# A Fourier convolution with a routed expert layer: the forward turns of batches 1 and 2 go through HBM

## The chip, the cores and the metric

The kernel runs on one core of a Trainium2 chip. A core has a matrix engine (PE, with its weight load shown as PEld), a vector engine (DVE), a scalar engine (ACT), a general engine (POOL) and a queue engine (SP) that here does nothing but issue transfers. They run side by side and wait for one another through semaphores; 16 DMA engines move data between HBM and the on-chip memory. The metric is the device time of one execution in microseconds (us): the median of three runs.

## What is computed

```python
def _attn_ref(x, filt_r, filt_i):                 # x: 8 batches x 3072 positions x 256 channels
    X = np.fft.rfft(x, axis=1)
    Y = X * (filt_r + 1j * filt_i)[None, :, :]
    return np.fft.irfft(Y, n=x.shape[1], axis=1)

def _moe_ref(x, w_gate, w1, w2, capacity):        # x: 24576 tokens x 256, 8 experts
    logits = x @ w_gate
    expert_idx = np.argmax(logits, axis=1)
    ...
    for i in range(N):                            # the first `capacity` = 768 tokens of an expert
        e = expert_idx[i]
        if counts[e] < capacity:
            disp[e, counts[e]] = x[i]; pos[i] = counts[e]; counts[e] += 1; keep[i] = True
    h = np.maximum(np.einsum('ecd,edf->ecf', disp, w1), 0.0)
    y = np.einsum('ecf,efd->ecd', h, w2)
    ...                                           # out[i] = gate_w[i] * y[expert, pos], else 0
```

Only the first 768 tokens of each of the 8 experts count, so the kernel convolves batches 0, 1 and 2 (the last in part) and turns to the experts; a branch that convolves everything stands behind them for inputs that need it.

## The kernel before

**The transform.** A batch has 3072 = 96 x 32 positions (n1, n2) and 256 channels. The forward transform over n1 is taken for eight **chunks** of four n2 each. `load_x` brings a chunk (96 partitions, 4 x 256 values, 384 KB) into a buffer `xt`, of which there are four. `a(c, h)` multiplies it on PE with the table `A` for one half h of the channels, and `a_out` copies the result on ACT into `ZA[h]`, which has the channels on its partitions. The second transform, over n2, wants (q, n2) on the partitions. `t(k)` makes it so: 16 PE transposes of `ZA` and two ACT copies into `Q`, six times in a batch. `Q` has 24 pairs of frequencies, 128 partitions x 256 channels each.

**The middle.** `middle` is the loop over six groups g of four pairs: `b(g, h)` (PE with table `Bc`, then two products with the filter on DVE and two sums on POOL), `g(u)` (PE with `IG`, a cast `yh` on ACT, a rest `yl` on DVE) and `bi(u)` (PE with `BIh`, `BIl`, copies into `V` on ACT). `g(0)` needs both halves of group 0 and stands behind the four `b` of groups 0 and 1. The argument `first` is a list of steps of which one runs behind each `b`; `fill` is a list of lists of which one runs at each filler, from group 1 on.

**The inverse and the routing.** `ai(V, dst, h)` returns the steps of the inverse transform: 11 for half 0 and 8 for half 1. I call the 8 of half 1 S0 to S7. Each has PE products, one ACT copy into a buffer `rt`, of which there are five, and a store of 153 or 192 KB to `ybuf`. `route` returns the lists `counts` (DVE, the last a scan), one PE step `sums` that waits for that scan, `slots` (DVE), four `masks` (DVE), and `table`: four PE steps, table 0 to 3, and a last one on DVE.

**The order.** It is written out by hand: every engine takes its instructions in the order in which the Python code calls them, and a wait holds up all that stands behind it on that engine. For b = 0 and 1 the loop calls the middle of batch b, then chunks 0 to 3 of batch b+1, the inverse of half 0, chunks 4 to 7 among `counts`, then `sums`, then the six `t` among `slots`, and then

```python
            run([masks[0], masks[1], S[0], S[1], table[0], masks[2], S[2], S[3], table[1], masks[3], S[4], S[5]])
            ahead = S[6:]
            fill = [[table[2]], table[3:]]
```

so S6 and S7 run inside the next middle, as `first`. I call the stretch from the end of a middle to the next one a **turn**; there are two. In the second turn `load_a` also brings 1 MB of expert 0's first weights into `raw`, and `cut_a` splits them on ACT in four pieces, from the first filler of the last middle on. All transfers named here but those of `cut_a` are issued by SP.

Of the kernel before, what the change touches and what calls it, by code (L numbers as in the profile page):

```python
# [9 lines left out]
F32 = mybir.dt.float32  # L10
# [11 lines left out]
N1, N2, NP = 96, 32, 24  # L22
# [67 lines left out]
def fftconv_moe_kernel(ctx, tc, x, x0, fr, fi, fny, wg, w1, w2, ca, cai, cb, co, out, cap):  # L90
    nc = tc.nc
    NB, SEQ, D = x.shape[0], N1 * N2, 256
# [4 lines left out]
    NB0 = min(NB, -(-E * cap // SEQ) + 1)  # L97
# [11 lines left out]
    dram = ctx.enter_context(tc.tile_pool(name="dram", bufs=1, space=bass.MemoryType.DRAM))  # L109
# [48 lines left out]
    def interleave(*lists):  # L158

        marks = sorted(((i + 1) / (len(l) + 1), j, i) for j, l in enumerate(lists) for i in range(len(l)))  # L160
        for _, j, i in marks:
            lists[j][i]()

    def run(fs):
        for f in fs:
            f()

    class Conv:
# [81 lines left out]
                f(self.A[k * 32:(k + 1) * 32, c, 32:4 * QP], t[N1:, k * w:(k + 1) * w])  # L250

        def load_x(self, b, c):
            t = self.side.tile([N1, 4, D], F32, name="xt", tag="xt")
            src = x[b] if isinstance(b, int) else x[bass.ds(b, 1)].rearrange("o c a t d -> (o c) a t d")
            nc.sync.dma_start(out=t, in_=src[c])
            self.xts[c] = t
# [541 lines left out]
    cv = Conv(p1b, top, side, True)  # L798
    route_tiles(p1b)

    with tc.manual_schedule():

        V = new_V(vp)
# [13 lines left out]
        ps = bank()  # L817
# [21 lines left out]
        fill, ahead = [[cv.finish_low]], [lambda: (cv.t(3), cv.t(4)), lambda: None, lambda: cv.t(5)]  # L839
        nz = -(-len(zfill) // (NB0 - 1))  # L840

        def with_zeros(fill, at):
            fill = [list(f) for f in fill] + [[] for _ in range(10 - len(fill))]
            for i in range(nz):
                fill[at[i % len(at)]].append(lambda: zero_out(1))
            return fill

        def rows_in(b, cs, more):
            steps = []
            for c in cs:  # L850
                steps += [lambda c=c: cv.a(c, 0), lambda c=c: cv.a(c, 1)]
                if more:
                    steps.append(lambda c=c: cv.load_x(b, c + 4))
            return steps

        for b in range(NB0 - 1):
            for c in range(4):
                cv.load_x(b + 1, c)
            cv.middle(V, with_zeros(fill, (3, 6)), ahead)
            L = new_L()  # L860
            halves = [ai(V, ybuf[b], h, L) for h in range(2)]
            counts, sums, slots, masks, table = route(L, False, (ohp, ohp))
            for q in range(4):
                ti(V, q)
            run(rows_in(b + 1, range(4), True))
            run(halves[0])
            interleave(rows_in(b + 1, range(4, 8), False), counts)
            sums()
            interleave([lambda k=k: cv.t(k) for k in range(NP // 4)], slots)
            if b + 2 == NB0:  # L870
                side_ctx.close()
                w0 = run_ctx.enter_context(tc.tile_pool(name="w0", bufs=1, side="right"))
                raw0 = run_ctx.enter_context(tc.tile_pool(name="raw0", bufs=1, side="right"))
                ep = run_ctx.enter_context(tc.tile_pool(name="ep", bufs=1, side="right"))
                (load_a, cut_a), (load_b, cut_b) = (load_part(0, part, raw0, w0, 4) for part in "ab")
                load_a()
            S = halves[1]
            run([masks[0], masks[1], S[0], S[1], table[0], masks[2], S[2], S[3], table[1], masks[3], S[4], S[5]])
            ahead = S[6:]
            fill = [[table[2]], table[3:]]  # L880


        b = NB0 - 1
        sm["p"] = ep
        last_fill = last_constants(ep)
# [14 lines left out]
        def early_row(e, t):  # L900
            gather(early_x[e][:, t:t + 1, :], idx0, e * NT + t, 1, b * SEQ)

        fill[0].append(cut_a[0])
        fill[1] += [early_index, cut_a[1]]
        fill += [[cut_a[2], lambda: early_row(0, 0)], [cut_a[3], load_b, lambda: early_row(0, 1)], [lambda: early_row(0, 2)], [last_fill],
                 [cut_b[0]], [cut_b[1]], [cut_b[2]], [cut_b[3], lambda: early_gate(0)]]
        cv.middle(V, fill, ahead, last=[early_turn])
        top_ctx.close()
# [94 lines left out]
        with tc.If(least < cap):  # L1003
            with ExitStack() as gp:
# [7 lines left out]
                V = new_V(p1b)  # L1012
# [91 lines left out]
```

## Time and profile before

| | us |
|---|---|
| median of 3 runs | 493.52 (492.25 to 494.03) |
| the profiled execution, its own time | 489.18 |
| its span, from the first to the last instruction | 487.5 |
| PE busy | 476.7 (98% of the span) |
| ACT busy | 269.3 (55%) |
| DVE busy | 239.7 (49%) |
| POOL busy | 199.9 (41%) |

The trace is of one execution, and its times are from the start of the span; 1.7 us lie around the span. Matmuls are pipelined, so a row's duration reaches a little into the next; the distance between the starts of two rows is what the first cost. A float32 product on PE counts as two instructions. TensorE's granted clock was 0.998 of full speed over the span.

### The profile page before, as it was taken

To read this page: it belongs to the slowest core of one execution; us is meant where nothing else is said; L and a number is where in the kernel's file an instruction comes from. 1 tells how busy PE (TensorE), PEld (TensorE's weight loads), DVE (VectorE), ACT (ScalarE), POOL (GpSimd) and SP (SyncE) were. 2 spreads that over 40 slices of the span, in tenths; PEclk is the share of its full clock that TensorE was granted. 3 is DMA by queue.
4 is the path that set the end of the run, shared out by engine and by line. 5 is a ranking of instruction groups with operands and counts; after the bars stand their busy time and mean duration, and the time that the engine had idled before them with its cause. 6 is when DMAs were issued, how large, how long until landed. Compare 5 with 4: busy or idle time off the path is not lost.

```text
span 487.5 us, 10394 instructions
## 1 busy us (share of the span) xinstructions
PE 476.7 (98%) x4078; PEld 469.7 (96%) x4078; DVE 239.7 (49%) x533; ACT 269.3 (55%) x626; POOL 199.9 (41%) x246
## 2 busy tenths in 40 slices
PE   8999999999999999999999999999999999999994
PEld 8999999999999999998999999999999999999994
DVE  3587755777737878956432342332322422423510
ACT  3555767456667677664362684392382572673411
POOL 3064210444100885617632654354463462563022
PEclk9999999999999999999999999999999999999999
DMA  8996180890546458385738599989989979984001
GB/s 292 377 323 263 34 233 5 218 377 13 162 107 190 88 154 185 82 227 99 222 73 234 128 240 267 356 231 260 364 216 271 378 191 278 374 162 107 0 24 48
DMA packets 60186, 95.70 MB, mean 196 GB/s; under 512 B 4224, under 2 KB 36704, under 8 KB 60000
## 3 DMA queue, kind: packets, MB, share of 16 engines
q1 hardware_dynamic: 43472, 63.28, 40.0%
q0 software_dynamic: 15344, 29.56, 28.1%
q10 hardware_dynamic: 1312, 2.10, 1.4%
q8 instruction: 34, 0.56, 0.5%
q14 instruction: 24, 0.20, 0.1%
HBM read 54.82 MB, written 40.11 MB: 195 GB/s over the span
## 4 chain that ended last, share of the span: by engine, by line
PE 73%; issue 10%; POOL 6%; ACT 4%; DMA 3%; DVE 2%; POOLq 0%; SPq 0%; DVEq 0%
PE ps L610 21%; PE ps L661 19%; PE ps L268 9%; PE ps L407 6%; PE ps L337 6%; PE ps L304 5%; PE ps L351 4%; POOL y L667 2%; DMA raw<-w 2%; PE ps L291 1%; PE ps L584 1%; POOL rows L570 1%; ACT Q L296 1%; DMA V<-x 1%; POOL wal L702 1%
## 5 line engine op out<-in xcount | busy, mean ns | idle before, releaser
L661 PE MATMUL ps<-wbh,h 128*128 128x256 f32 x768 | 139.6, 282 | 0.0
L593 DVE SCALAR_TENSOR_TENSOR h<-ps,h 128x384 fp32r<-128x384 f32 x128 | 67.0, 552 | 109.0 <-ACT h L591 108.7
L661 PEld LDWEIGHTS ps<-wbh,h 128*128 128x128 f32 x768 | 118.9, 189 | 0.8 <-issue 0.4
L661 PE MATMUL ps<-wbl,h 128*128 128x256 f32 x384 | 107.6, 280 | 0.0
L667 POOL DMA_INDIRECT y<-ob,idxs x48 | 48.1, 1003 | 115.7 <-ACT ob L664 110.5
L610 PE MATMUL ps<-xl,wah 128*128 128x384 f32 x256 | 86.4, 338 | 0.3 <-DVE xl L595 0.2
L610 PE MATMUL ps<-xh,wah 128*128 128x384 f32 x256 | 86.5, 338 | 0.0
L610 PE MATMUL ps<-xh,wal 128*128 128x384 f32 x256 | 86.2, 337 | 0.0
L591 ACT ACTIVATE h<-ps 128x384 fp32r<-128x384 f32 x128 | 58.8, 497 | 33.7 <-PE ps L610 32.5
L661 PEld LDWEIGHTS ps<-wbl,h 128*128 128x128 f32 x384 | 72.5, 189 | 0.0
L664 ACT ACTIVATE ob<-ps,gt 128x256 f32<-128x256 f32 x48 | 22.7, 475 | 85.4 <-PE ps L661 45.7
L324 POOL TENSOR_TENSOR t<-t,t 128x256 f32<-128x256 f32 x33 | 24.9, 754 | 68.3 <-DVE t L320 44.3
L570 POOL DMA_INDIRECT rows<-ybuf,idxg x42 | 42.4, 1009 | 16.3 <-issue 11.0
L610 PEld LDWEIGHTS ps<-xl,wah 128*128 128x128 f32 x256 | 48.0, 188 | 0.9 <-DVE xl L595 0.9
L610 PEld LDWEIGHTS ps<-xh,wah 128*128 128x128 f32 x256 | 48.0, 188 | 0.2
L610 PEld LDWEIGHTS ps<-xh,wal 128*128 128x128 f32 x256 | 48.0, 188 | 0.0
L595 DVE TENSOR_TENSOR xl<-ps,xh 128x384 fp32r<-128x384 f32 x32 | 16.2, 547 | 46.9 <-ACT xh L591 46.9
L340 ACT CAST yh<-ps 128x408 fp32r<-128x408 f32 x48 | 23.9, 502 | 27.7 <-PE ps L337 26.2
L337 PE MATMUL ps<-IG,t 128*128 128x136 f32 x288 | 38.2, 281 | 0.9 <-POOL t L325 0.9
L337 PEld LDWEIGHTS ps<-IG,t 128*128 128x128 f32 x288 | 35.4, 190 | 1.5 <-POOL t L325 1.5
L304 PE MATMUL ps<-Bc,Q 128*128 128x128 f32 x288 | 35.8, 276 | 0.0
L304 PEld LDWEIGHTS ps<-Bc,Q 128*128 128x128 f32 x288 | 33.8, 192 | 0.1
(134 smaller groups left out, 766.9 us busy)
## 6 DMA issues: line engine op xcount, KB each, us to landing
y<-zt SPq DMA_DIRECT2D x12, 2048.0 KB, 22.0
raw<-w SPq DMA_DIRECT2D x13, 1024.0 KB, 9.9
wbl<-w POOLq DMA_DIRECT2D x16, 512.0 KB, 12.2
wal<-w POOLq DMA_DIRECT2D x14, 512.0 KB, 7.5
xt<-x SPq DMA_DIRECT2D x16, 384.0 KB, 5.2
ybuf<-rt SPq DMA_DIRECT2D x16, 192.0 KB, 2.9
ybuf<-rt SPq DMA_DIRECT2D x20, 153.0 KB, 2.5
Q<-x SPq DMA_DIRECT2D x4, 528.0 KB, 8.9
```

Source lines behind the costliest of these rows:

```text
L268: nc.tensor.matmul(ps[:, i * w:(i + 1) * w], xt[:, i, h * 128:(h + 1) * 128], A[:, i * QP:i * QP + w], start=True, stop=True)
L304: nc.tensor.matmul(ps[:, i * 128:(i + 1) * 128], self.Q[:, p, h * 128:(h + 1) * 128], self.Bc[:, 1 if p == NP - 1 else 0, :], start=True, ...
L324: eng.tensor_tensor(out=t1[:, :, 0, :], in0=t1[:, :, 0, :], in1=t2[:, :, 1, :], op=ALU.subtract)
L337: nc.tensor.matmul(ps[:, i * 136:(i + 1) * 136], self.ysb[(p // 4, h)][:, (p % 4) * 128:(p % 4 + 1) * 128], self.IG[:, h, :], start=True, ...
L340: nc.scalar.copy(fh[:, o], ps[:, :408])
L407: nc.tensor.matmul(ps[:N1, i * w:(i + 1) * w], AI[:, n0 + i, :], V[h][:, :w // 2, n0 + i, :], start=True, stop=True)
L570: nc.gpsimd.indirect_dma_start(out=rows[:, t, :], out_offset=None, in_=yrows[:lim, :], in_offset=bass.IndirectOffsetOnAxis(ap=idx[:, j + t ...
L591: nc.scalar.activation(out=hi, in_=ps, func=AF.Relu if relu else AF.Copy)
L593: nc.vector.scalar_tensor_tensor(out=lo, in0=ps, scalar=0.0, in1=hi.bitcast(F32), op0=ALU.max, op1=ALU.subtract)
L610: nc.tensor.matmul(ps[:, :n * 128], w[:, kk, m * 128:(m + 1) * 128], y[:, kk, o], start=k == 0, stop=k == 5)
L661: nc.tensor.matmul(ps[:, :D], y[:, m, o], w[:, m, :], start=m == 0 and j == 0, stop=m == NF - 1 and j == 2)
L667: ins = nc.gpsimd.indirect_dma_start(out=out, out_offset=bass.IndirectOffsetOnAxis(ap=(idxs if ix is None else ix)[:, j:j + 1], axis=0), i ...
```

## The change

Batches 1 and 2 lose the transposes. `a_rows(c)` multiplies with the operands exchanged, so that the result has q on its partitions and the 256 channels in a row; two ACT copies of 96 x 512 bring it into one of three slots of the former `ZA[0]`, and SP stores it to a new HBM buffer `zturn`. Chunk 7 is stored in two pieces. Seven loads of `Q` read `zturn` back with (q, n2) on the partitions, two of two pairs and five of four. I call them Q0 to Q6. Chunks 4 to 6 of the input are loaded into slots of the former `ZA[1]`, so all input but chunk 7 can be loaded during the middle before. S6 and S7 move ahead of the middle; table 2, table 3 and the last table step become `ahead`. `sums` stands behind two chunks instead of four. `load_a` stands behind Q3 and S5, where it was ahead of S0. The zero stores of the output move from the fillers 3 and 6 to 5 and 7.

```diff
         def load_x(self, b, c):
-            t = self.side.tile([N1, 4, D], F32, name="xt", tag="xt")
+            if self.resident and 4 <= c < NCH - 1:
+                t = self.slot(1, c - 4).rearrange("p (t d) -> p t d", d=D)
+            else:
+                t = self.side.tile([N1, 4, D], F32, name="xt", tag="xt")
...
+        def slot(self, h, k):
+            return self.ZA[h].rearrange("p q t -> p (q t)")[:N1, k * 4 * D:(k + 1) * 4 * D]
+
+        def a_rows(self, c):
+
+            xt, A, z = self.xts.pop(c), self.Ac[c], self.slot(0, c % 3)
+            for k in range(2):
+                ps = bank()
+                for i in range(2):
+                    t = 2 * k + i
+                    nc.tensor.matmul(ps[:QP, i * D:(i + 1) * D], A[:, t * QP:(t + 1) * QP], xt[:, t, :], start=True, stop=True)
+                nc.scalar.copy(z[:, k * 2 * D:(k + 1) * 2 * D], ps[:QP, :])
+                if k or c == NCH - 1:
+                    o = slice(2 * k if c == NCH - 1 else 0, 2 * k + 2)
+                    nc.sync.dma_start(out=zturn[:, c * 4 + o.start:c * 4 + o.stop, :],
+                                      in_=z[:, o.start * D:o.stop * D].rearrange("p (t d) -> p t d", d=D))
+
+        def load_Q(self, p, n):
+
+            src = zturn[p * 4:(p + n) * 4].rearrange("(p j) t c -> (j t) p c", p=n)
+            nc.sync.dma_start(out=self.Q[:, p:p + n, :], in_=src)
...
-            run(rows_in(b + 1, range(4), True))
+            run(rows_in(b + 1, range(4)))
             run(halves[0])
-            interleave(rows_in(b + 1, range(4, 8), False), counts)
+            interleave(rows_in(b + 1, range(4, 6)), counts)
             sums()
-            interleave([lambda k=k: cv.t(k) for k in range(NP // 4)], slots)
+            interleave(rows_in(b + 1, range(6, 8)), slots)
...
-                load_a()
             S = halves[1]
...
+            first = [load_a] if b + 2 == NB0 else []
+            run([Q[0], Q[1], masks[0], masks[1], S[0], S[1], table[0], masks[2], S[2], Q[2], S[3], table[1], masks[3], S[4], Q[3], S[5]] + first + S[6:])
+            ahead = [table[2], lambda: run(table[3:])]
+            fill = []
+            loads = Q[4:]
```

SP's order in the second turn, from the last forward work to the end of the turn, stood before like this (the `raw` row is `load_a`, the 96x4x128 rows are the stores of S0 to S7, `both` is a small constant):

```order
L695 DMA raw<-w 128x2x1024 [waits DVE_49,PE_49,DMAHW7_49,Activation_49,Pool_49]
L413 DMA ybuf<-rt 96x4x128 [waits DMAHW0_49,Activation_49]
L413 DMA ybuf<-rt 96x4x128 [waits DMAHW1_49,Activation_49]
...
L763 DMA both<-co 128x144 [waits DMAHW6_49]
L413 DMA ybuf<-rt 96x4x128 [waits DMAHW7_49,Activation_49]
L413 DMA ybuf<-rt 96x4x128 [waits DMAHW0_49,Activation_49]
```

and in the changed kernel, from the second piece of chunk 7 on (`zturn<-ZA`), it stands like this:

```order
L292 DMA zturn<-ZA_97 96x512 [waits DMAHW7_49,Activation_49]
L298 DMA Q<-zturn 128x2x256 [waits DMAHW5_49,DMAHW6_49,DMAHW4_49,DMAHW7_49,DMAHW3_49,DMAHW0_49]
L298 DMA Q<-zturn 128x2x256 [waits DMAHW1_49]
L439 DMA ybuf<-rt 96x4x128 [waits DMAHW2_49,Activation_49]
L439 DMA ybuf<-rt 96x4x128 [waits Activation_49] x2
L298 DMA Q<-zturn 128x4x256
L439 DMA ybuf<-rt 96x4x128 [waits Activation_49] x2
L298 DMA Q<-zturn 128x4x256 [waits DMAHW0_49]
L439 DMA ybuf<-rt 96x4x128 [waits DMAHW1_49,Activation_49]
L721 DMA raw<-w 128x2x1024 [waits DMAHW2_49,PE_49]
L439 DMA ybuf<-rt 96x4x128 [waits DMAHW3_49,Activation_49]
L439 DMA ybuf<-rt 96x4x128 [waits DMAHW4_49,Activation_49]
```

`load_a` went from ahead of the eight stores to behind four loads of Q and six stores, and all of them stand behind a load that waits for the stores of the last chunks (the DMAHW names).

On PE, the end of the first turn and the start of the middle stood before like this (L407 are steps S, L304 is `b`, L550 a table, L337 `g(0)`):

```order
L407 MATMUL ps<-V_117,AI 96x128 x8
L304 MATMUL ps<-Bc,Q 128x128 x8
L407 MATMUL ps<-V_117,AI 96x128 x4
L304 MATMUL ps<-Bc,Q 128x128 x4
L407 MATMUL ps<-V_117,AI 96x128 x4
L550 LDWEIGHTS ol
L550 MATMUL pr<-ohh,ol 128x96
...
L304 MATMUL ps<-Bc,Q 128x128 x4
L337 MATMUL ps<-IG,t_1272 128x136
```

and the same place in the changed kernel (L433, L330, L576 and L363 are the same four):

```order
L433 MATMUL ps<-V_118,AI 96x128 x16
L330 MATMUL ps<-Bc,Q 128x128 x8
L576 LDWEIGHTS ol
L576 MATMUL pr<-ohh,ol 128x96
...
L330 MATMUL ps<-Bc,Q 128x128 x4
L576 LDWEIGHTS ol
L576 MATMUL pr<-ohh,ol 128x96
...
L330 MATMUL ps<-Bc,Q 128x128 x4
L363 MATMUL ps<-IG,t_1139 128x136
```

Two steps S left the place between the first `b` and `g(0)`, and one more table came into it.

## Rows read from the trace of the kernel before

**Rows 1.** Page, first part: busy time, share of the span, instructions by engine.

```profile
PE 476.7 (98%) x4078; PEld 469.7 (96%) x4078; DVE 239.7 (49%) x533; ACT 269.3 (55%) x626; POOL 199.9 (41%) x246
```

**Rows 2.** Stretches: length, busy PE, PEld, DVE, ACT, POOL, then granted clock, DMA share, GB/s.

```profile
144.30:148.90 4.60, 4.18 (x102) 3.69 (x101) 3.98 (x16) 3.82 (x9) 0.00 (x0) 1.00 0.00 0
190.80:487.00 296.20, 289.82 (x2252) 285.75 (x2250) 111.00 (x274) 149.82 (x296) 131.04 (x128) 1.00 0.75 201
```

**Rows 3.** Timeline of PE, first turn: start, duration, instructions [idle before, released by].

```profile
56.34 7.31 PE L268 MATMUL ps<-A,xt 96*128 96x128 f32 x64
63.48 7.62 PE L407 MATMUL ps<-V,AI 128*96 128x136 f32 x64
70.95 7.31 PE L268 MATMUL ps<-A,xt 96*128 96x128 f32 x64
78.09 0.26 PE L495 MATMUL pr<-sc,tri 96*96 96x8 f32 x2
...
78.45 3.43 PE L291 MATMUL ps<-ident,ZA 64*128 64x64 f32 x81
...
82.74 2.00 PE L407 MATMUL ps<-V,AI 128*96 128x128 f32 x16
84.58 0.51 PE L550 MATMUL pr<-ohh,ol 96*128 96x96 f16 x8
...
88.87 1.95 PE L304 MATMUL ps<-Bc,Q 128*128 128x128 f32 x16
...
94.61 1.55 PE L337 MATMUL ps<-IG,t 128*128 128x136 f32 x12
```

**Rows 4.** Timeline of DVE, first turn: the scan that `sums` waits for.

```profile
74.12 0.69 DVE L491 TENSOR_TENSOR_SCAN sc<-mask,oh 96x256 f32<-96x256 f32 x1
```

**Rows 5.** Timeline of ACT, start of the last middle.

```profile
155.17 0.58 ACT L409 COPY rt<-ps 96x512 f32<-96x512 f32 x1 [0.30 <-PE ps L407]
...
160.08 0.62 ACT L700 CAST wah<-raw 128x512 fp32r<-128x512 f32 x1
160.60 0.63 ACT L704 ACTIVATE wal<-raw 128x512 fp32r<-128x512 f32 x1
161.56 0.50 ACT L340 CAST yh<-ps 128x408 fp32r<-128x408 f32 x1 [0.33 <-PE ps L337]
```

**Rows 6.** Timeline of DVE, last middle: the last table step and what follows it.

```profile
163.29 0.20 DVE L555 TENSOR_TENSOR tacc<-tacc,pr 128x48 f32<-128x48 f32 x1
...
163.90 0.15 DVE L782 TENSOR_TENSOR tot<-tot,lack 128x2 f32<-128x2 f32 x1
```

**Rows 7.** Timeline of PE, second turn and last middle.

```profile
122.39 2.84 PE L268 MATMUL ps<-A,xt 96*128 96x128 f32 x24
...
160.67 1.56 PE L337 MATMUL ps<-IG,t 128*128 128x136 f32 x12
...
170.35 0.50 PE L337 MATMUL ps<-IG,t 128*128 128x136 f32 x2 [0.46 <-POOL t L325]
```

**Rows 8.** Stretches (columns as in Rows 2): rates of single kinds of transfer.

```profile
150.00:151.00 1.00, 1.00 (x17) 0.98 (x15) 0.20 (x1) 1.00 (x4) 0.00 (x0) 1.00 1.01 135
88.00:90.00 2.00, 2.00 (x21) 2.00 (x20) 0.53 (x3) 1.16 (x2) 0.00 (x0) 1.00 1.02 270
266.00:267.00 1.00, 1.00 (x11) 1.00 (x10) 0.83 (x4) 0.83 (x3) 0.00 (x0) 1.00 1.07 341
267.00:268.00 1.00, 1.00 (x11) 1.00 (x10) 0.87 (x4) 0.07 (x1) 0.00 (x0) 1.00 1.06 372
242.00:243.00 1.00, 1.00 (x11) 1.00 (x10) 0.00 (x0) 0.00 (x0) 0.55 (x1) 1.00 1.01 414
30.00:32.00 2.00, 2.00 (x20) 2.00 (x19) 1.75 (x4) 0.97 (x3) 1.77 (x3) 1.00 1.03 256
```

**Rows 9.** SP's timeline at `load_a`, and the landing times of L413's 38 stores.

```profile
149.01 0.41 SPq L695 DMA_DIRECT2D raw<-w  x1
...
DMA to landing us min/median/max: 2.2/2.7/7.9
```

More of the change, by code (lines that the diff above doesn't have):

```diff
@@ L114, in fftconv_moe_kernel @@
     yall = dram.tile([NB, N1, N2, CH], F32, name="yall")
+    zturn = dram.tile([4 * NP, N2, D], F32, name="zturn")
     yrows = ybuf.rearrange("b a t c -> (b a t) c")
@@ L846, in with_zeros, with rows_in @@
             return fill
-        def rows_in(b, cs, more):
+        def rows_in(b, cs):
             steps = []
             for c in cs:
-                steps += [lambda c=c: cv.a(c, 0), lambda c=c: cv.a(c, 1)]
-                if more:
-                    steps.append(lambda c=c: cv.load_x(b, c + 4))
+                steps.append(lambda c=c: cv.a_rows(c))
+                if c == 0:
+                    steps.append(lambda: cv.load_x(b, NCH - 1))
             return steps
+        loads = []
         for b in range(NB0 - 1):
-            for c in range(4):
-                cv.load_x(b + 1, c)
-            cv.middle(V, with_zeros(fill, (3, 6)), ahead)
+            loads += [lambda b=b, c=c: cv.load_x(b + 1, c) for c in range(NCH - 1)]
+            fill = with_zeros(fill, (5, 7))
+            for i, f in enumerate(loads):
+                fill[i // 2].append(f)
+            cv.middle(V, fill, ahead)
             L = new_L()
@@ L875, in fftconv_moe_kernel @@
                 (load_a, cut_a), (load_b, cut_b) = (load_part(0, part, raw0, w0, 4) for part in "ab")
-                load_a()
             S = halves[1]
-            run([masks[0], masks[1], S[0], S[1], table[0], masks[2], S[2], S[3], table[1], masks[3], S[4], S[5]])
-            ahead = S[6:]
-            fill = [[table[2]], table[3:]]
+            Q = [lambda p=p, n=n: cv.load_Q(p, n) for p, n in ((0, 2), (2, 2), (4, 4), (8, 4), (12, 4), (16, 4), (20, 4))]
+            first = [load_a] if b + 2 == NB0 else []
[3 more added lines that the diff above has]
+            loads = Q[4:]
         b = NB0 - 1
@@ L901, in early_row @@
             gather(early_x[e][:, t:t + 1, :], idx0, e * NT + t, 1, b * SEQ)
-        fill[0].append(cut_a[0])
-        fill[1] += [early_index, cut_a[1]]
-        fill += [[cut_a[2], lambda: early_row(0, 0)], [cut_a[3], load_b, lambda: early_row(0, 1)], [lambda: early_row(0, 2)], [last_fill],
+        fill = [[loads[0], cut_a[0]], [early_index, cut_a[1]] + loads[1:], [cut_a[2], lambda: early_row(0, 0)],
+                [cut_a[3], load_b, lambda: early_row(0, 1)], [lambda: early_row(0, 2)], [last_fill],
                  [cut_b[0]], [cut_b[1]], [cut_b[2]], [cut_b[3], lambda: early_gate(0)]]
```

## The prediction

> **What bounds the kernel now.** The first part of the page has PE busy for 98% of the span [rows 1], at a granted clock of 1.00 in all stretches used here [rows 2, 8]. From 190.8 on PE is idle for 6.4 us of 296, most of it the tail behind its last product [rows 2], so what a turn wins on PE's timeline moves the end by as much. I then read PE's timeline of the first turn; the second repeats it 66.05 later, with the same 4.18 of 4.60 busy in its transposes [rows 2, 3, 7]. Read from start to start: chunks 0 to 3 take 7.14, the inverse of half 0 7.47, chunks 4 to 7 7.14, `sums` 0.36, the transposes 4.29, S0 to S5 with two tables 6.13, and from the first `b` to `g(0)` 5.74 [rows 3]. There is hardly a gap, so only work taken off PE, or a wait put on it, counts. One more place matters: in the last middle PE waits 0.46 at 170.35 for a POOL sum [rows 7]; there POOL and DVE set the pace, not PE.
>
> The sum is made on the profiled execution (489.18, span 487.5). It ran 0.9% below the median of 493.52; I subtract its microseconds from the median, since nothing in the sum depends on that difference.
>
> **Part by part, first turn** (times from its start at 56.34).
>
> Transposes removed: 4.29 of PE. Their 12 ACT copies hide behind that today and go with them.
>
> Operands exchanged: per chunk 4 products of 256 columns instead of 8 of 128, the same number of columns. A product needs at least its columns, so the change lies between nothing and the issue cost saved. No row has 256 float32 columns. I take 0.1 per four chunks, 0.2 in a turn (0 to 0.4). ACT's two copies of 96 x 512 cost 0.58 each [rows 5], under the 1.76 that PE needs per chunk, so they hide. A slot comes round after three chunks (5.3), a store lands 2.2 to 2.7 after its issue [rows 9] (those are half as large; 1 more at most), so the slots hide too.
>
> `sums` moved up: PE comes to it at 7.04 + 7.47 + 3.52 = 18.03. The scan it needs ends at 18.47 [rows 4], less the 0.1 saved ahead of it. PE waits 0.34. Nothing hides this, because chunks 6 and 7 are queued behind.
>
> S6 and S7 moved out of the middle: they cost PE 1.84 [rows 3] wherever they stand, but they filled the start of the middle. `g(0)` waits for POOL's sums of group 0, which come after four DVE products in series: 5.74 behind the first `b`. PE's work in that time was four `b`, S6, S7 and table 2. Six steps S at 0.92 leave 0.6 of the 6.13 for two tables, so a table is 0.3 and the four `b` are 3.6. Now it is four `b` and two tables, 4.2, and PE waits 1.54 for POOL.
>
> Sum of the first turn: 4.29 + 0.2 - 0.34 - 1.54 = 2.6 gained, if the loads of Q come in time. Chunk 7 leaves PE at 18.37 + 0.36 + 3.52 = 22.25, its last copy ACT at 22.83. Its store lands about 2.6 later [rows 9], with two more pieces right ahead of it at 256 GB/s, the rate of 96-partition tiles in rows of 4 KB [rows 8]: 25.4. SP then issues Q0. From issue to full DMA share takes 0.95 (149.01 to about 150) [rows 8, 9]. For the rate of Q the nearest row is the load of w2, also in rows of 1 KB: 341 and 372, so 356 [rows 8]. Q0 and Q1 (0.52 MB) take 1.47. From last byte to semaphore I put 0.67 (the shortest store, 2.2, less 0.95 and 0.58 for 157 kB at 270). They land at 28.5; `b` comes at 22.25 + 6.13 + 1.84 = 30.22, so 1.7 are to spare. Q2 stands behind S0 to S2, 0.197 MB each at 270 [rows 8], and lands at 32.2, when `b` of group 1 comes (32.3). Q3 lands at 35.1, ahead of the end of `g(0)` at 37.4 (start 35.96 as below, and the row's 1.55, less a little for its overlap). SP holds the stores of S0 and later until chunk 7 has landed; with five `rt`, S5's copy waits for S0's store (29.2), but PE has seven banks and `yh` comes only at 36.9.
>
> **Second turn.** The same, with 2.6, but `load_a` now stands behind Q0 to Q3 and S0 to S5. These are 1.57 MB at 356, 1.18 MB at 270 and 1.05 MB at 414 (w1 in rows of 4 KB) [rows 8]: 4.42 + 4.37 + 2.56 = 11.35 from 26.35 on, and 0.67 to land, 38.4. The first piece of `cut_a` is queued on ACT ahead of the first two `yh`. Without a wait the `yh` would start 0.89 behind the start of `g(0)` (35.96), at 36.85, so ACT should reach `raw` well before it has landed. Behind ACT stand `yl` on DVE, the index work, the products of group 2, POOL's sums with a gather between them, and the last part of `g(2)`, the product that waits today. In the trace this chain takes 8.79 from the start of `yh` to 170.35 [rows 5, 7]; the table step of 0.61 that stood in it [rows 6] now comes earlier, so 8.18. The two ACT operations of the cut take 1.15 [rows 5]. So `g(2)` goes on at 38.4 + 1.15 + 8.18 = 47.7, against 170.35 - 122.39 = 47.96 today [rows 7]: 0.2 gained instead of 2.6. The gain of the second turn is nearly eaten by the wait for `raw`.
>
> Bounds: with all transfers at 414, 3.80 MB take 9.2, `raw` lands at 36.2 and the turn gains 2.4. With Q at 256, the slowest row of a large load, it lands at 40.1 and the turn loses 1.5. I take 356 because the size of the rows is the same. Input loads and zero stores go on in the middle behind Q; even at 256 GB/s, the lowest rate of a large transfer in the rows, they end before the next turn (2.75 MB of input in 10.7, in a middle of 33.5, 88.87 to 122.39), so I cost them at nothing. Were they late, they would delay the first stores of a turn, which nobody waits for until the slot comes round.
>
> The rows give a store or load a fixed part of 0.95 + 0.67 = 1.6, twice in series here. The Trainium skill ("DMA: Bandwidth & Descriptors", section "Anatomy of one DMA") gives about 2.0 us for it, most of it the receipt of the last write. By that rule `raw` would land 0.8 later and the sum would be 2.1 instead of 2.8, 491.4. The shortest landing here, 2.2 with its data [rows 9], is below what the rule gives for that size (2.4), so the row stands.
>
> Forecast: 2.6 + 0.2 = 2.8, so 493.52 - 2.8 = **490.7**.
>
> **The rivals.**
>
> *`raw` comes early.* If the queue drains faster, or ACT comes to the cut later than I think, only PE's own waits remain: `g(2)` goes on at 36.85 + 8.18 = 45.0, and both turns gain, 2.6 + 2.9 = 5.5: 488.0. It needs `raw` by 35.7. Speaks for it: 414 GB/s exists in the trace [rows 8]. Against: the stores in rows of 512 B, a third of the bytes, run at 270 [rows 8].
>
> *The loads of Q run at half the rate, and it gets slower.* They read rows that were written microseconds ago, among stores; no row shows such a read. At 178 GB/s Q0 to Q3 take 8.84, `raw` lands at 42.8, `g(2)` goes on at 52.1: 4.2 lost in the second turn. In the first, Q2 lands at 35.1 and Q3 at 39.5, which delays `g(0)` by 1.2 and group 2 by 0.9, leaving 0.5. Sum 3.7 lost: 497.2. It decides at about 225 GB/s, where both turns cancel.
>
> *The stores to the new buffer are slow.* If they ran at 128 instead of 256 GB/s, the last four (1.57 MB, from 17.8 on) would land at 30.8, 5.4 late; the first turn would lose 1.1 and the second 5.2: 499.8. Rows of a store lie 32 KB apart there. The Trainium skill ("DMA: Bandwidth & Descriptors", section "Latency and other measured facts") reports such a loss for row distances at large powers of two, from 2 MiB on, while 512 KiB still ran at the full rate. No run so far shows a store with such distances.
>
> *Nothing comes of it.* If POOL's pace, or a wait on `rt` or on a slot, takes back the 2.6 in both turns, the time stays at 493.5.
>
> **How the numbers follow.** Forecast with its bounds (489.0 to 493) 0.55; `raw` early (487.2 to 489) 0.20; Q slow 0.13; stores slow 0.05; nothing 0.07. The range is 487.2 to 495.5: it takes in the first two and the last, and of the slow cases the mildest. A measurement of this kernel can tell 0.5%, 2.5 us, from no change, and the forecast lies at that edge: 0.55 of its own case is beyond it. Faster: 0.20 + 0.30 = 0.50. Slower: most of the two slow cases, less what stays under 496, and nothing else, 0.13. The same: 0.37.
>
> **What would show it.** In the trace after: no transposes after batch 0's; `sums` with a wait of about 0.3; a PE wait of about 1.5 before each of the two `g(0)`; Q0 issued about 25.4 into a turn; the first `wah` of the last middle waiting for the DMA of `raw`, until about 38.4 into its turn; and `g(2)` there with a wait of some 2 us. Wrong would be: `b` waiting for Q (my rate or the landing of chunk 7 is off), or no ACT wait for `raw` (then the time is near 488).

## The result, and the profile after

The changed kernel takes 498.81 us (497.74 to 499.49, four runs) against 493.5 before: a ratio of 1.0098, 95% interval 1.0075 to 1.0120. The medians differ by 5.3 us, and the interval stands for 3.7 to 5.9 more, where a gain of 2.8 was forecast; the time lies outside the stated range of 487.2 to 495.5. One profile below, e4's, is of an execution slower than the others of its kernel, and no reading rests on it.

The first line of the page, and the cores' view (span, mean granted clock), which for the kernel before gave 487.5 and 0.998:

```profile
PE 476.1 (96%) x3758; PEld 459.0 (92%) x3758; DVE 240.2 (48%) x533; ACT 261.2 (52%) x602; POOL 200.1 (40%) x246
core 0: 497.8 us, clock 0.986
```

PE is busy for about as long as before [rows 1], with 320 instructions fewer. So work was taken away, and waits and a lower clock came in.

The first turn on PE's timeline, to be held against [rows 3]:

```profile
56.26 7.07 PE L288 MATMUL ps<-xt,A 96*96 96x256 f32 x32
63.16 7.62 PE L433 MATMUL ps<-V,AI 128*96 128x136 f32 x64
70.62 3.62 PE L288 MATMUL ps<-ZA,A 96*96 96x256 f32 x16
75.72 0.34 PE L521 MATMUL pr<-sc,tri 96*96 96x8 f32 x2 [1.48 <-DVE sc L517]
...
76.08 2.33 PE L288 MATMUL ps<-ZA,A 96*96 96x256 f32 x8
78.20 3.24 PE L288 MATMUL ps<-xt,A 96*96 96x256 f32 x8
...
89.09 1.95 PE L330 MATMUL ps<-Bc,Q 128*128 128x128 f32 x16
...
93.07 1.13 PE L330 MATMUL ps<-Bc,Q 128*128 128x128 f32 x8 [1.69 <-DMA Q<-zturn]
94.04 0.51 PE L576 MATMUL pr<-ohh,ol 96*128 96x96 f16 x8
94.39 1.86 PE L330 MATMUL ps<-Bc,Q 128*128 128x128 f32 x8
96.04 2.51 PE L363 MATMUL ps<-IG,t 128*128 128x136 f32 x12
```

Two waits stand here, 1.48 ahead of `sums` (L521) and 1.69 ahead of the `b` of group 1 (L330). Behind each the same work takes longer than it should. The two chunks from 70.62 on take 3.62, and the next two 5.20, from 76.08 to 81.28 (where L433 starts again); one half of a `b` takes 0.97 from 93.07 on, and the next 1.65 from 94.39 on. The view by stretches says why (columns as in [rows 2]; the column before the last two is the granted clock):

```profile
74.30:75.70 1.40, 0.00 (x0) 0.00 (x0) 1.29 (x3) 0.56 (x1) 0.00 (x0) 1.00 0.84 244
76.10:77.50 1.40, 1.40 (x9) 1.08 (x9) 1.17 (x6) 0.30 (x1) 0.00 (x0) 1.00 0.67 208
77.60:80.80 3.20, 3.20 (x9) 2.06 (x9) 2.96 (x12) 1.34 (x3) 0.00 (x0) 0.50 0.31 81
81.10:84.10 3.00, 3.00 (x33) 2.93 (x32) 1.22 (x4) 1.75 (x3) 0.00 (x0) 1.00 0.49 146
91.40:93.00 1.60, 0.00 (x0) 0.00 (x0) 1.26 (x3) 0.58 (x1) 0.99 (x2) 1.00 1.09 325
94.70:97.40 2.70, 2.70 (x15) 2.70 (x13) 2.47 (x7) 0.00 (x0) 1.48 (x3) 0.50 1.16 317
145.90:149.00 3.10, 3.10 (x8) 1.98 (x7) 2.86 (x13) 1.17 (x2) 0.00 (x0) 0.50 0.41 116
```

TensorE's granted clock falls to 0.50, its 1.2 GHz level, 1 to 2 us after PE has started again, and comes back to 1.00 after some 3.4. It happens twice in the first turn and once in the second. Added up over half-microsecond stretches, each such phase costs 1.71. In the stretches that I read in the trace of before it was 1.00 throughout [rows 2, 8].

The second turn starts at 124.36. Rows of PE, then the first row of the cut on ACT, then the last part of `g(2)` on PE:

```profile
143.76 0.34 PE L521 MATMUL pr<-sc,tri 96*96 96x8 f32 x2 [1.42 <-DVE sc L517]
161.03 1.13 PE L330 MATMUL ps<-Bc,Q 128*128 128x128 f32 x8 [1.60 <-DMA Q<-zturn]
...
166.97 0.62 ACT L726 CAST wah<-raw 128x512 fp32r<-128x512 f32 x1 [6.84 <-DMA raw<-w]
...
175.79 0.50 PE L363 MATMUL ps<-IG,t 128*128 128x136 f32 x2 [0.99 <-POOL t L351]
...
194.48 0.58 PE L610 MATMUL ps<-ident,rows 64*128 64x64 f32 x12
```

The last row, the first transposes of the expert part, serves as a mark: from the start of a turn to the next start, or to this mark, gives the lengths of the two turns, each with the middle behind it. Before they are 66.05 and 66.64 (the mark is at 189.03), after 68.10 and 70.12: +2.05 and +3.48, together +5.53. That is near the difference of the medians. The remaining 4.8 by which the two profiled spans differ lies behind the mark, where nothing was edited. I come to that first.

### The profile page after: what moved, and what is told of

It is laid out like the page before. It is cut to its first block, busy times and chain, and to the rows that moved or that the text cites. A ratio compares the mean times of both kernels' runs of the same rounds, so it can differ in the third digit from the quotient of the medians.

```text
span 497.8 us, 9802 instructions
## 1 busy us (share of the span) xinstructions
PE 476.1 (96%) x3758; PEld 459.0 (92%) x3758; DVE 240.2 (48%) x533; ACT 261.2 (52%) x602; POOL 200.1 (40%) x246
## 4 chain that ended last, share of the span: by engine, by line
PE 53%; issue 20%; POOL 10%; DMA 7%; DVE 4%; ACT 3%; SPq 1%; POOLq 1%; ACTq 0%; DVEq 0%
PE ps L636 13%; PE ps L687 12%; PE ps L363 5%; PE ps L288 5%; PE ps L330 4%; PE ps L377 4%; POOL y L693 4%; PE ps L433 4%; PE ps L272 3%; POOL rows L596 3%; DMA ybuf<-rt 3%; DMA raw<-w 2%; POOL wal L734 1%; DMA Q<-zturn 1%; PE ps L848 1%
## 5 line engine op out<-in xcount | busy, mean ns | idle before, releaser
L330 PE MATMUL ps<-Bc,Q 128*128 128x128 f32 x288 | 36.7, 280 | 4.3 <-DMA Q<-zturn 3.3
L363 PE MATMUL ps<-IG,t 128*128 128x136 f32 x288 | 39.2, 285 | 1.4 <-POOL t L351 1.4
L330 PEld LDWEIGHTS ps<-Bc,Q 128*128 128x128 f32 x288 | 34.5, 195 | 4.9 <-ACT rt L435 3.5
L363 PEld LDWEIGHTS ps<-IG,t 128*128 128x128 f32 x288 | 36.4, 195 | 2.1 <-POOL t L351 2.0
```

What stands on the lines that cost most here:

```text
L330: nc.tensor.matmul(ps[:, i * 128:(i + 1) * 128], self.Q[:, p, h * 128:(h + 1) * 128], self.Bc[:, 1 if p == NP - 1 else 0, :], start=True, ...
L363: nc.tensor.matmul(ps[:, i * 136:(i + 1) * 136], self.ysb[(p // 4, h)][:, (p % 4) * 128:(p % 4 + 1) * 128], self.IG[:, h, :], start=True, ...
```

## The experiments

All kernels but two start from the changed one. Lengths of turns are read from one profile each, as above; the ratios are from timed runs, each against the kernel before on the same chip:

| kernel | turn 1 | turn 2 | ratio to before (95%) |
|---|---|---|---|
| before, first and second profile | 66.05, 66.05 | 66.64, 66.66 | |
| changed, first and second profile | 68.10, 68.26 | 70.12, 71.20 | 1.0098 (1.0075 to 1.0120) |
| e1 `sums` behind three chunks, and e14 the same again | 63.78, 63.20 | 67.18, 67.45 | 0.9987 (0.9961 to 1.0014) |
| e2 13 products of zeros | 70.50 | 70.14 | 1.0158 (1.0111 to 1.0205) |
| e10 6 products of zeros | 65.05 | 69.01 | 1.0065 (1.0041 to 1.0089) |
| e3 chunk 7 loaded later | 68.82 | 71.70 | 1.0180 (1.0127 to 1.0233) |
| e11 without that load | 67.26 | 69.16 | |
| e6 before, steps moved alone | 67.29 | 67.29 | 1.0022 (1.0000 to 1.0043) |
| e5 e1, later cut, S6 and S7 in the middle | 62.96 | 67.99 | 1.0005 (0.9980 to 1.0030) |
| e7 e1, later cut, Q0 to Q3 together | 67.01 | 70.91 | 1.0110 (1.0071 to 1.0148) |
| e8 e1, `load_a` behind Q2 | 63.23 | 65.50 | 0.9998 (0.9971 to 1.0025) |
| e9 e8, S6 and S7 in the middle, and e15 the same again | 62.90, 63.08 | 71.17, 70.13 | 0.9951 (0.9934 to 0.9968), 0.9988 (0.9962 to 1.0014) |
| e12 the same with Q3 ahead of `load_a` | 63.80 | 70.45 | 0.9996 (0.9973 to 1.0019) |

**How much is steady: e0, e13, e14.** The kernel before and the changed one, without an edit.

> The kernel before, unchanged, profiled once more. In the first profile of it the span was 487.5, some 4 below what the timed runs imply, and from the last middle to the end it has hardly a PE wait; the profile of the changed kernel has some 4 us more of waits in that stretch, which no edit touches. Theory: that part differs from execution to execution, so this profile may show waits there too (span 488 to 492), while the two turns stay at 66.05 from start to start. Rival: the late waits come from the change; then this profile repeats 487.5 with no such waits.

Measured: the turns repeat to 0.02, and the part behind the mark is 3.15 longer, with waits such as this one, which the first profile lacked:

```profile
420.13 0.44 PE L610 MATMUL ps<-xh,wah 128*128 128x384 f32 x1 [1.31 <-ACT ob L664]
```

So the expert part differs from execution to execution: behind the mark the seventeen profiles read here, e4's left out, spread from 297.9 to 305.7, in no order that follows the edits. Single spans can't be compared; the turns are steadier. But a turn is also read from one execution, and a phase of half clock comes in some executions and not in others: e9's two turns add up to 1.38 more than before, and its timed ratio is 0.9951. Where a ratio is near 1, the timed runs decide, not the turns.

> The changed kernel, unchanged, profiled once more, on the same chip as the next. Theory A (the waits at `sums` and at the `b` of group 1 are in the order of the work, so they come in each execution; whether the clock falls behind a given wait is not): the two turns again take 67 to 71 each, with waits of 1.4 to 1.5 at `sums` and 1.6 or more at `b`, and the half clock behind most of them. Rival (the first profile caught a bad execution): a sum of the two turns under 135 instead of 138.2.

> The kernel with `sums` behind three chunks, profiled once more. Theory A: the two turns again near 63.8 and 67.2, without a half clock behind `sums`. Rival: they are as long as those of the changed kernel, 68 and 70.

Measured: 68.26 and 71.20 for the changed kernel, with waits of 1.55 and 1.44 at `sums`, 1.70 and 1.65 at `b`, and four phases of half clock instead of three; 63.20 and 67.45 for the other, without one. The loss is steady and no bad draw.

**`sums` one chunk later: e1.**

```diff
-            interleave(rows_in(b + 1, range(4, 6)), counts)
+            interleave(rows_in(b + 1, range(4, 7)), counts)
             sums()
-            interleave(rows_in(b + 1, range(6, 8)), slots)
+            interleave(rows_in(b + 1, range(7, 8)), slots)
...
-            run([Q[0], Q[1], masks[0], masks[1], S[0], S[1], table[0], masks[2], S[2], Q[2], S[3], table[1], masks[3], S[4], Q[3], S[5]] + first + S[6:])
+            run([Q[0], Q[1], masks[0], masks[1], S[0], S[1], S[2], table[0], masks[2], Q[2], S[3], S[4], table[1], masks[3], Q[3], S[5]] + first + S[6:])
```

> The changed kernel with `sums` behind three chunks instead of two, and the first two tables one step S later, so that their one-hot masks are there. Theory A (one chain of dominoes: PE waits 1.45 at `sums`, the granted clock then falls to half for about 3.4 us, chunk 7 is stored 3 us late, so the loads of Q and of `raw` come 3 us late): no wait at `sums`, no half clock there, the first load of Q issued at about 25.4 into a turn instead of 28.1, the wait of `b` for Q under 0.3; time 489 to 492. Rival B (the loads of Q are too slow whenever they start): the wait at `b` grows by what `sums` gives back; 496 to 499.

Measured: this edit takes the ratio from 1.0098 to 0.9987, so the loss is gone, and no gain over the kernel before is shown. PE's timeline, first turn (start 57.71), then second (start 121.49):

```profile
77.90 0.34 PE L521 MATMUL pr<-sc,tri 96*96 96x8 f32 x2 [0.48 <-DVE sc L517]
...
91.87 1.13 PE L330 MATMUL ps<-Bc,Q 128*128 128x128 f32 x8 [1.35 <-DMA Q<-zturn]
...
155.03 1.13 PE L330 MATMUL ps<-Bc,Q 128*128 128x128 f32 x8 [1.59 <-DMA Q<-zturn]
...
170.00 0.50 PE L363 MATMUL ps<-IG,t 128*128 128x136 f32 x2 [1.00 <-POOL t L351]
```

The wait at `sums` is 0.48 and none, the clock stays at 1.00 in both turns, and Q0 is issued 25.52 and 24.76 into a turn instead of 28.12 and 27.96. Rival B was half right: `b` still waits 1.35 and 1.59 for Q. But it didn't grow by what `sums` gave back, and it costs little, since `g(0)` follows the first `b` by 6.04 and 6.16, where POOL's sums alone make it 5.74.

**Is it the clock? e2 and e10.** Products of zeros, never read, in the place of the wait at `sums`, 13 of them and then 6:

```diff
+            warm_wait(6)
             sums()
```

> The changed kernel with 13 products of zeros (128 columns each, about 1.4 us, their result is never read) on PE in the place where it waits for the scan ahead of `sums`. Theory A, its part on the clock (what the wait costs beyond its own 1.45 is the half clock of some 3.4 us behind it, 1.7 a turn): `sums` comes at the same time as in the changed kernel, the clock stays at 1.00 behind it, chunks 6 and 7 take 3.5 instead of 5.2, the first load of Q is issued 1.7 earlier; 491 to 495. Rival (chunks 6 and 7 are slow for another reason, the copies or the stores of the slots): they take 5.2 again, and the time is that of the changed kernel or above it, 498 to 500.

> The changed kernel with 6 products of zeros instead of 13 ahead of `sums`: in the run with 13 one of them took 0.22, twice what was planned, so that PE came to `sums` 1 to 2 late. 6 of them are 1.3 of the 1.45 that PE waits. Theory A on the clock: no half clock behind `sums`, chunks 6 and 7 in 3.5, the first turn 1.5 to 3 shorter than the changed kernel's 68.1. Rival: the clock falls to half there all the same, or the turn is as long without it.

13 were too many: a product took 0.22, so they pushed `sums` back by 1.3 in each turn. The chunks behind it took 3.5 and the clock stayed at 1.00 there, but Q0 was issued as late as in the changed kernel, or later. In the first turn `b` then waited 2.60 for Q, and the clock fell there for twice as long as in the phases above. The kernel got slower; the time was missed. With 6, PE's timeline and the clock around `sums` (L853 are the zeros):

```profile
74.22 1.50 PE L853 MATMUL ps<-zt 128*128 128x128 f32 x12
75.66 0.34 PE L521 MATMUL pr<-sc,tri 96*96 96x8 f32 x2
...
76.02 1.95 PE L288 MATMUL ps<-ZA,A 96*96 96x256 f32 x8
77.80 1.89 PE L288 MATMUL ps<-xt,A 96*96 96x256 f32 x8
```

```profile
77.60:80.80 3.20, 3.20 (x22) 2.72 (x21) 2.96 (x12) 2.01 (x5) 0.00 (x0) 1.00 0.43 123
```

`sums` comes no later than in the changed kernel, the two chunks take 3.51, and the turns are 3.05 and 1.11 shorter. The 1.11 is the cleaner number: in the first turn the phase behind `b` is missing as well, although `b` waits 2.19 there, longer than the 1.69 of the changed kernel. The ratio goes to 1.0065; its interval overlaps a little with that of the changed kernel. Useless work in the place of a wait made the kernel faster in the profile: it is the clock that makes the wait at `sums` so dear.

**What makes the scan late: e3 and e11.** In the changed kernel the scan ends 19.41 into the turn (74.98 and 0.69), where 18.37 was forecast. ACT's timeline shows where the delay begins:

```profile
66.86 0.49 ACT L435 COPY rt<-ps 96x408 f32<-96x408 f32 x1 [0.20 <-PE ps L433]
69.28 1.04 ACT L435 COPY rt<-ps 96x408 f32<-96x408 f32 x2 [1.92 <-DMA ybuf<-rt]
```

The sixth copy into the five `rt` waits 1.92 for the first store; the copies of the logits, the reduce and the scan follow. I took the load of chunk 7 for the cause, moved it behind the fifth store (e3), and then left it out (e11).

```diff
-            run(halves[0])
+            run(halves[0][:5])
+            cv.load_x(b + 1, NCH - 1)
+            run(halves[0][5:])
```

> The changed kernel with the load of input chunk 7 issued behind the fifth store of the inverse's half 0 instead of behind chunk 0. Theory A, its first domino (the scan is late because ACT waits 1.9 at the sixth copy into `rt` for the first store, which stands behind 1.57 MB of chunk stores and the 0.39 MB of this load): that wait falls to about 0.5, the scan comes some 0.9 earlier, PE waits about 0.6 at `sums`, and with it less or none of the half clock: 492 to 496. Rival (the store is late by the chunk stores alone): ACT waits 1.5 or more again, 497 to 500.

> The changed kernel without the load of input chunk 7 in the turns: chunk 7 is computed from the input of chunk 0, so its part of the result is left out. Only the two turns are looked at. Theory A, first domino (ACT waits at the sixth copy into `rt` because 1.57 MB of chunk stores and the 0.39 MB of this load stand ahead of the first store on the DMA engines): the wait falls from 1.9 to 0.5 or less, the scan comes 0.8 to 1.2 earlier in the turn, and PE waits 0.3 to 0.6 at `sums`. Rival (the stores alone are too much): ACT waits 1.5 or more.

The rival holds, but for a small part. Without the load (e11, first turn, start 56.52) the sixth copy still comes after a gap of 1.61, and `sums` waits 1.14 instead of 1.48. In the kernel before (start 56.34) the same copy waited 0.40. The first two rows are e11's, the last is of the kernel before:

```profile
67.13 0.49 ACT L435 COPY rt<-ps 96x408 f32<-96x408 f32 x1 [0.20 <-PE ps L433]
69.23 1.03 ACT L435 COPY rt<-ps 96x408 f32<-96x408 f32 x2 [1.61 <-PE ps L433]
...
68.08 1.05 ACT L409 COPY rt<-ps 96x408 f32<-96x408 f32 x2 [0.40 <-DMA ybuf<-rt]
```

The second row names PE, but PE ran without a gap there, and the other thing that this copy needs is a free `rt`, which the first store gives. With the load moved (e3) the sixth copy waits 1.59, the tenth and the eleventh wait as well, and `sums` waits 2.21 and 2.57. What is left are the chunk stores. How busy the DMA engines are does not explain e11's wait: before, four loads of chunks, as many bytes, went ahead of the first store, and the share was about the same (the kernel before, e11, the changed kernel; DMA share and GB/s in the last two columns):

```profile
64.00:68.00 4.00, 4.00 (x36) 4.00 (x36) 2.01 (x1) 2.64 (x6) 1.00 (x5) 1.00 0.88 248
64.00:68.00 4.00, 4.00 (x37) 4.00 (x36) 2.28 (x2) 2.75 (x6) 1.00 (x5) 1.00 0.85 239
64.00:68.00 4.00, 4.00 (x37) 4.00 (x36) 2.00 (x1) 2.48 (x6) 1.00 (x5) 1.00 0.91 262
```

What differs is what SP issues right ahead of the first store, and how long ahead (the kernel before, then e11):

```profile
63.67 0.31 SPq L255 DMA_DIRECT2D xt<-x  x1
64.91 0.33 SPq L413 DMA_DIRECT2D ybuf<-rt  x1
...
64.30 0.30 SPq L292 DMA_DIRECT2D zturn<-ZA  x1
64.85 0.32 SPq L439 DMA_DIRECT2D ybuf<-rt  x1
```

The last load went 1.24 ahead of the first store, the last chunk store goes 0.55 ahead of it. That the chunk stores hold up the first store is what remains after e3 and e11; it is argued, not shown. A kernel without these stores, or with more `rt`, was not run.

**The steps alone: e6.** The kernel before, with its transposes; S6 and S7 go ahead of the middle, tables 2 and 3 into it.

> The kernel before, with its transposes, and one part of the change alone: S6 and S7 ahead of the middle, tables 2 and 3 inside it. Expected from the trace of before: PE waits 1.5 for POOL ahead of `g(0)` in each turn, 3.1 in all at full clock, so 1.006 of the kernel before; up to 1.7 more a turn where the clock falls to half behind the wait, 1.013. Rival: PE finds other work or the wait is hidden; 1.000.

Measured: PE waits for POOL, as the forecast has it, but for 0.87 and 0.60, and the turns are 1.24 and 0.65 longer; 1.0022. The first row of `g(0)`, two products that could already run, is what I had left out:

```profile
91.84 1.95 PE L304 MATMUL ps<-Bc,Q 128*128 128x128 f32 x16
...
96.24 0.50 PE L337 MATMUL ps<-IG,t 128*128 128x136 f32 x2
97.60 1.43 PE L337 MATMUL ps<-IG,t 128*128 128x136 f32 x10 [0.87 <-POOL t L325]
```

From the first `b` to the end of the wait it is 5.76, the forecast's 5.74. Here the clock did not fall.

**The queue in front of the middle: e4, e5, e7, e8, e9, e12, e15.** These start from e1 and move what is queued. `cut_a` later:

```diff
-        fill = [[loads[0], cut_a[0]], [early_index, cut_a[1]] + loads[1:], [cut_a[2], lambda: early_row(0, 0)],
-                [cut_a[3], load_b, lambda: early_row(0, 1)], [lambda: early_row(0, 2)], [last_fill],
+        fill = [[loads[0]], [early_index, cut_a[0]] + loads[1:], [cut_a[1], lambda: early_row(0, 0)],
+                [cut_a[2], cut_a[3], load_b, lambda: early_row(0, 1)], [lambda: early_row(0, 2)], [last_fill],
```

> The kernel with `sums` behind three chunks, and on top of it the four pieces of `cut_a` start one filler later (the second to fourth filler, two pieces in the last of them), so that ACT comes to the first `yh` of the last middle before it comes to `raw`. Theory A (of the second turn's loss what is left is ACT held 6.9 by `raw` ahead of `yh`): no ACT wait ahead of the first `yh`, the last part of `g(2)` goes on some 45.5 us into the second turn instead of 48.5, and the time falls by 2.5 to 3.5 against the kernel with `sums` moved alone: 487 to 488. Rival: the pace of POOL and DVE holds group 2 anyway, 490 to 491.

Measured: 1.0019 (0.9993 to 1.0045), a miss.

S6 and S7 back in the middle, Q2 with Q0 and Q1:

```diff
+            run([Q[0], Q[1], Q[2], masks[0], masks[1], S[0], S[1], S[2], table[0], masks[2], S[3], S[4], table[1], masks[3], Q[3], S[5]] + first)
+            ahead = S[6:]
+            fill = [[table[2]], table[3:]]
```

> The last kernel with S6 and S7 back inside the middle, as `first` (tables 2 and 3 at its first two fillers), and Q2 issued with Q0 and Q1 ahead of all stores of S. Theory A (the products `b` come 1.84 earlier; `g(0)` follows the first `b` by 5.74 because of POOL, and PE has 1.84 of work in that gap): if Q0 lands by 28.5 and Q2 by 32 in a turn, `g(0)` comes 1.0 to 1.8 earlier in both turns, 484 to 486. Rival (the loads of Q set the start, since chunk 7 is stored no earlier): `b` waits 1 to 2 for Q0 and Q2 and the time is that of the kernel without it, 487 to 488.

Measured: the first turn falls to 62.96, the second stays at 67.99, and the time does not fall (1.0005). It also suggests why the later cut gained nothing. ACT has the first `yh` ahead of it now, and still waits:

```profile
159.85 0.62 ACT L726 CAST wah<-raw 128x512 fp32r<-128x512 f32 x1 [3.16 <-DMA raw<-w]
...
163.09 2.48 PE L330 MATMUL ps<-Bc,Q 128*128 128x128 f32 x16 [2.20 <-DVE yl L367]
```

The second pair of `yh` is late instead of the first, PE waits 2.20, and the clock falls to half.

> The kernel with `sums` and `cut_a` moved, and on top of it Q0 to Q3 issued together, ahead of the stores of S0 and later. Theory A (Q2 stands behind three stores, so it lands 1.4 to 1.9 later than `b` of group 1 comes): the wait of `b` for Q falls from about 1.5 to under 0.4, but a wait of about 1.2 for POOL's sums ahead of `g(0)` takes its place, since `g(0)` stands 5.74 behind the first `b` anyway; the time falls by 0.3 to 0.8, within what can be told. Rival (Q2 is late because loads of Q run slowly, not because of its place): `b` waits 1 or more for Q again.

Measured: the wait of `b` for Q falls to 0.63 and none, as expected, and a wait of 0.17 and 0.60 for POOL takes its place. But the kernel gets slower (1.0110): the stores of S now stand behind four loads, ACT waits for an `rt`, and SP comes late to `raw` and to Q4 to Q6. The rows are two of PE and, between them, two of ACT in the second turn:

```profile
100.23 3.27 PE L330 MATMUL ps<-Bc,Q 128*128 128x128 f32 x16 [2.10 <-DMA Q<-zturn]
...
157.50 1.27 ACT L435 COPY rt<-ps 96x512 f32<-96x512 f32 x2 [6.46 <-DMA ybuf<-rt]
...
166.39 0.62 ACT L726 CAST wah<-raw 128x512 fp32r<-128x512 f32 x1 [5.79 <-DMA raw<-w]
...
169.60 3.37 PE L330 MATMUL ps<-Bc,Q 128*128 128x128 f32 x16 [5.23 <-DVE yl L367]
```

In the first turn PE waits 2.10 for Q4; in the second ACT waits for `rt`, then for `raw`, and PE waits 5.23 for what hangs on it.

Then `load_a` behind Q2 (e8), with S6 and S7 in the middle besides (e9, e15), and Q3 ahead of it (e12). The order of e8:

```diff
+            run([Q[0], Q[1], masks[0], masks[1], S[0], S[1], S[2], table[0], masks[2], Q[2]] + first + [S[3], S[4], table[1], masks[3], Q[3], S[5]] + S[6:])
```

> The kernel with `sums` behind three chunks, `cut_a` where the change has it, and `load_a` issued right behind Q2, ahead of Q3 and of the stores of S3 to S5. Theory A (what is left of the second turn's loss is ACT held by `raw`, which stands behind 1.1 MB that could follow it): `raw` lands at 36 to 37 into the second turn instead of 39.7, the ACT wait ahead of the first `yh` falls to under 0.5, the second turn takes 64 to 65 instead of 67.2, 0.992 to 0.995 of the kernel before in time. Rival: Q3, now behind `raw`, comes late for group 2 and takes the gain back, 67 again and 0.999.

Measured: ACT goes on with `raw` 36.24 into the second turn (start 119.79), its wait halves, and the last part of `g(2)` waits only 0.26. The row of ACT:

```profile
156.03 0.62 ACT L726 CAST wah<-raw 128x512 fp32r<-128x512 f32 x1 [3.26 <-DMA raw<-w]
```

So `raw` comes earlier as expected, and the turn is 65.50, in spite of a phase of half clock from 153.5 on. In this one profile the two turns are 4.0 shorter than before. The timed runs do not show that gain (0.9998).

> On top of that S6 and S7 inside the middle again, Q2 issued with Q0 and Q1, `load_a` behind S1. With S6 and S7 beside the first `b` alone the first turn took 62.96 against 63.78. Theory A: 63 and 63 to 64 for the two turns, so 5.5 to 6.5 below the kernel before, 0.987 to 0.990. Rival (each load that moves up moves another back: Q3, or the stores that free `rt`): one of the two turns takes 66 or more.

> The kernel with S6 and S7 in the middle and `load_a` behind S1 once more, beside the one with Q3 ahead. Before, it took 0.995 of the kernel before. Theory A: 0.993 to 0.997 again, the first turn 63, and the second with a wait of 2 to 3.5 for Q3. Rival: 0.998 or more, the first result was the chip's.

> The kernel with S6 and S7 in the middle and `load_a` behind S1, with Q3 ahead of `load_a` (there Q3 came late and PE waited 3.5 for it in the second turn). Theory A (the queue carries 3.8 MB between the last chunk and group 2, and what stands last is late): the wait for Q3 goes, ACT waits 2 to 3 more for `raw`, the second turn takes 65 to 67 and the first 63; 0.990 to 0.994 of the kernel before. Rival: the wait for `raw` takes back all of it; 0.995 or more.

The order of e9 and e15, and that of e12:

```diff
+            run([Q[0], Q[1], Q[2], masks[0], masks[1], S[0], S[1]] + first + [S[2], table[0], masks[2], S[3], S[4], table[1], masks[3], Q[3], S[5]])
...
+            run([Q[0], Q[1], Q[2], masks[0], masks[1], S[0], S[1], Q[3]] + first + [S[2], table[0], masks[2], S[3], S[4], table[1], masks[3], S[5]])
```

Measured: the first turns are 62.90, 63.08 and 63.80; the second ones 71.17, 70.13 and 70.45. In e9 and e15 PE waits 3.46 and 4.49 for Q3, as the rival has it; with Q3 ahead (e12) it waits 0.98 for `yh` and then 1.75 for Q4. The row of PE in e9:

```profile
161.45 2.02 PE L330 MATMUL ps<-Bc,Q 128*128 128x128 f32 x16 [3.46 <-DMA Q<-zturn]
```

What moves up in the queue moves another load back. The ratio of 0.9951 did not come again on another chip (0.9988, 0.9962 to 1.0014), so none of these kernels is shown to beat the kernel before.

## Why the prediction was wrong

**The bound.** PE was and is the bound, and what is taken off or put on its timeline moved the end by as much: +5.53 in the turns, +5.3 in the medians. For this change that step held.

**Transposes and operands.** They are gone with their 4.29. Four chunks take 6.90 instead of 7.14, so 0.24 for each four where 0.1 was put; the chunks' slots in `ZA` held nothing up.

**`sums`: the step that failed.** The forecast took the time of the scan from the trace of before, 18.47 less 0.1, and put the wait at 0.34. The scan ends at 19.41, since ACT, ahead of it, waits for `rt` (1.92 at the sixth copy, 0.40 before), most likely behind the stores of the chunks, which are new. I had looked for `rt` in the second half of the inverse only. PE waits 1.48 and 1.42. That is 1.1 more in a turn.

**The clock, which the sum had as 1.00.** Behind the wait at `sums` it falls to half and costs another 1.71. So the term of 0.34 was in truth 3.2. The last copy of chunk 7 ends at 25.85 instead of 22.83, Q0 is issued at 28.12 instead of 25.4, `b` waits for Q, and in the first turn the clock falls again, another 1.71. It did so there in both profiles of the changed kernel, but not in e3, e10 and e11, where `b` waited about as long or longer, so this second fall is not shown to follow from `sums`. The first turn adds up: 2.6 forecast, less 1.14, 1.71 and 1.71, is a loss of 1.96; measured 2.05.

**S6 and S7.** The PE wait of 1.54 for POOL was replaced by one of 1.69 for Q, ahead of the `b` of group 1, so the term stood at its size by luck. Alone, in e6, the move costs 1.24 and 0.65: the term was too large by the part of `g(0)` that runs ahead.

**The loads of Q.** With `sums` out of the way (e1) Q0 is issued at 25.52 and 24.76, as forecast; the `b` that needs Q2 goes on at 34.16 and 33.54, where Q2 was put at 32.2. The rate was near: 325 GB/s from 91.4 to 93.0, with stores among it, where 356 was put. The stores of S3 and S4, issued behind Q2 while it is still under way, I had left out of the sum. In e1's second turn 2.16 MB moved from 147.2 to 155.0, when `b` goes on, and only 1.64 MB stands in SP's order from Q0 to the end of Q2. The rival with half the rate is excluded.

**The stores.** The second piece of chunk 7 is issued at 82.14 and Q0, which waits for it, at 84.38: 2.24, where the forecast had about 2.6 from the last copy. So the rival of slow stores falls, and a row distance of 32 KB cost nothing that shows. The Trainium skill ("DMA: Bandwidth & Descriptors", section "Anatomy of one DMA") would give an estimate of 2.45 for these 196 kB, on a path that is not SP's, which the prediction did not say; the row is below it, and it decides.

**The second turn.** The mechanism was named: ACT stands at `raw`, and `g(2)` goes on late behind it. `raw` came at 42.61 instead of 38.4; 2.6 of that is Q0's delay by `sums`. The other 1.6 is a size that was off: in e1 and e14, without that delay, `raw` came at 39.69 and 39.93, and from the issue of Q0 it took 14.9 in both, where 13.0 was put. Two stretches of e1's second turn, up to `b` and up to `raw`, show the bytes:

```profile
147.20:155.00 7.80, 6.24 (x66) 6.07 (x64) 4.70 (x10) 2.91 (x5) 1.30 (x2) 1.00 0.99 277
147.20:161.10 13.90, 12.31 (x124) 12.15 (x123) 7.72 (x17) 2.91 (x5) 5.60 (x8) 1.00 1.03 306
```

Until `raw` landed, 4.25 MB moved at 306 GB/s, where the sum had 3.80 MB at 335; so 0.45 MB that does not stand ahead of `raw` passed before it. From `raw` to `g(2)` it took 8.82, where 9.33 was put. `g(2)` goes on at 51.43, 3.7 after the forecast's 47.7, and the turn loses 3.48 where 0.2 were to be gained.

With the one wait removed, e1 and e14 give -2.27 and -2.85 in the first turn and +0.54 and +0.81 in the second, for the forecast's -2.6 and -0.2. So one step, the time of the scan, together with the clock behind its wait, turned the sign. Of the rest, `raw` was sized too small, S6 and S7 came out by luck, and whether what remains is a gain is not shown by the timed runs (0.9987, 0.9961 to 1.0014).

That the clock fell in e8 at 153.5, behind a wait of 1.75, and not in e10, behind waits of 2.19 and 2.25 in the same place, remains without an explanation here, and so does e8's missing gain in the timed runs.

## What to carry to other kernels

When a step is moved ahead, the time at which its input is ready must be worked out in the new order, with the new transfers, down to the buffers that the input's chain needs; the trace of before gives it for the old order only. A wait on a saturated PE can cost more than its length, because the clock may fall behind it: price a wait of 1 to 2 us there at up to 1.7 more, and treat its place, not only its length, as a risk. Where one queue carries all that the next stage waits for, moving one load up moves another back, so first count the bytes that pass before each of them is needed, some of those issued behind it included.

## What was not expected of the hardware

The granted clock fell to its lower level behind waits far shorter than I would have feared, and not behind others that were longer. In fifteen profiles (all but e4's and the two of the kernel before, each from the first turn to the last middle) there are eight waits at `sums` of 1.13 to 2.57, and behind or in seven of them the clock fell. Of 27 waits of `b` for Q, 1.24 to 4.49 long, it fell behind or in seven; a wait of 3.46 is among the other twenty. A phase cost 1.71. Three lasted twice as long (in e2, e3 and e15), and in these three the clock had fallen while PE still waited. Ahead of `sums` PE does the products of the chunks, ahead of `b` the products of the steps S and of `b`; whether that makes the difference was not tried.
